# Strassen's scheme for one more product, with its weight sums spread over two engines: an attention and SiLU kernel on one core

## The chip, the cores and the metric

One core of a Trainium2 chip. The metric is the device time of one execution in microseconds (us). The changed kernel and each experiment were executed six times, beside executions of the kernel before on the same chip; medians are quoted with the lowest and the highest. Profiled spans are about 2 us shorter than the device time of the same execution.

## The reference, cut to what matters

```python
# q, k, v: (8 items, 8 heads, 576, 64), float32; w_in (512, 2048), w_out (2048, 512)
q_s = softmax(q, axis=-1)                      # over the 64 of a head
k_s = softmax(k, axis=2)                       # over the 576 positions
kv  = einsum('bhsd,bhse->bhde', k_s, v)
x   = einsum('bhsd,bhde->bhse', q_s, kv)       # -> 4608 tokens x 512
h   = x @ w_in                                 # first product
g   = h * sigmoid(h)
out = g @ w_out                                # second product
```

The 4608 tokens go through the two products in nine chunks of 512 (the first product of chunks 0 and 1 has another cut: 576 and 448 tokens). An item is 576 tokens of attention; the attention of item b stands beside chunk b-1.

## The kernel before: the parts that matter

Instructions are put at positions in a chunk by a hand-tuned table, `PLAN`, sorted, and issued in that order on each engine. Chunks 3 to 7 share one entry, `STEADY`. The first product of chunk 0 and 1 is plain; from chunk 2 on it is partly, and the second product wholly, by Strassen's scheme: seven products of half blocks in place of eight, with sums of weights (`TX` for the first product, `TW` for the second) and of activations (`XS`, `SW`) made beforehand. Second products of chunks 0 and 1 are plain:

```python
def mm2(t, i):                       # a quarter product: 4 matmuls of 128x512
    qd, tb = divmod(i, 4)
    ...
    for fc in range(qd * n, (qd + 1) * n):
        nc.tensor.matmul(out=OP[t, tb], lhsT=GT[t][:, fc, tb*128:(tb+1)*128], rhs=W2[:, fc, :], ...)
    if qd == 3:
        store(t, tb, tb % 2)

y1 = [(t, x) for t in (1, 2) for x in PLAN[t]["y"]]     # chunk 1's 16: nine in chunk 1, seven in chunk 2
for i, (t, x) in enumerate(y1):
    put(t, x, mm2, 1, i)
```

The way of one item's queries into the products: load (`lq`), exponential on ScalarE (`ex`), row sums on VectorE, normalization on GpSimd (`qnorm`), a transposition by DMA (`tp`), and then the head products on TensorE (`ox`), whose copies are the next chunk's input.

```python
put(b - 1, p["qn"][cc], qnorm, b, cc, G)                # G: GpSimd
put(b - 1, p["vs"][cc], vcast, b, cc, V if b == 1 else G)
put(b - 1, p["lq"], load, b + 1, "qt", q)               # the next item's loads and
put(b - 1, p["lk"], load, b + 1, "kt", k)               # this item's transposition and the
put(b - 1, p["lv"], load, b + 1, "vt", v)               # output stores all are issued on one
put(b - 1, p["tp"], tr_dma, b, nc.sync)                 # queue, SyncE's, in this order of positions
```

The softmax here doesn't subtract the row's maximum and nothing guards it: scores larger than these inputs give would overflow.

## Time and profile before

The kernel before took 275.68 us (median of 3; 275.18 to 276.43) and, beside the changed kernel, 276.06 us (275.18 to 277.79, six runs). Its profiled span is 274.1 us. I cut it where TensorE begins each chunk's first product; the last column ends with the last matmul, 4.9 us before the span does:

| chunk | 0 | 1 | 2 | 3 | 4 | 5 | 6 | 7 | 8 to the last matmul |
|---|---|---|---|---|---|---|---|---|---|
| before, us | 33.01 | 23.39 | 21.30 | 28.06 | 27.85 | 28.89 | 27.12 | 25.75 | 37.34 |

```profile
57.36 0.54 SPq L98 DMA_DIRECT2D qt<-in_q_dram  x1
61.71 3.30 SPq L138 DMA_TRANSPOSE qT<-eq  x1
```

The transposition of item 2 is issued at 61.71 us and lands 4.9 us later, at 66.6. So item 2's head products could not have begun before 66.6: of the 5.2 us of quarter products ahead of them, at most 2.1 us cost time.

### The profile page before, as it was taken

To read this page: it belongs to the slowest core of one execution; us is meant where nothing else is said; L and a number is where in the kernel's file an instruction comes from. 1 tells how busy PE (TensorE), PEld (TensorE's weight loads), DVE (VectorE), ACT (ScalarE), POOL (GpSimd) and SP (SyncE) were. 2 spreads that over 40 slices of the span, in tenths; PEclk is the share of its full clock that TensorE was granted. 3 is DMA by queue.
4 is the path that set the end of the run, shared out by engine and by line. 5 is a ranking of instruction groups with operands and counts; after the bars stand their busy time and mean duration, and the time that the engine had idled before them with its cause. 6 is when DMAs were issued, how large, how long until landed. Compare 5 with 4: busy or idle time off the path is not lost.

```text
span 274.1 us, 6282 instructions
## 1 busy us (share of the span) xinstructions
PE 261.6 (95%) x2546; PEld 186.8 (68%) x2546; DVE 218.1 (80%) x417; ACT 167.8 (61%) x268; POOL 70.4 (26%) x53
## 2 busy tenths in 40 slices
PE   8789999999999999999999979999999999999992
PEld 3447665444446567877787668768876887788882
DVE  2957578995786999899889988989898679687932
ACT  5646663775995798378936695499554447444300
POOL 1551080579881008001700170015200000000000
PEclk9979999999999999999999999999999999999998
DMA  7999999998707970697099707951513012201414
GB/s 249 303 193 255 324 299 179 397 333 184 301 0 162 315 284 8 130 378 248 2 129 345 275 13 146 384 200 31 117 48 79 1 41 53 66 13 28 115 41 115
DMA packets 42381, 46.48 MB, mean 170 GB/s; under 512 B 18544, under 2 KB 29808, under 8 KB 42352
## 3 DMA queue, kind: packets, MB, share of 16 engines
q1 hardware_dynamic: 37312, 38.35, 47.4%
q0 software_dynamic: 5040, 7.73, 12.6%
q8 instruction: 20, 0.33, 0.5%
q14 instruction: 9, 0.07, 0.1%
HBM read 36.70 MB, written 9.44 MB: 168 GB/s over the span
## 4 chain that ended last, share of the span: by engine, by line
PE 61%; DMA 12%; ACT 8%; DVE 8%; SPq 4%; issue 3%; POOL 2%; ACTq 0%; POOLq 0%; DVEq 0%
PE ops L410 21%; PE hps L234 16%; PE hps L317 14%; DMA kt<-in_k_dram 9%; PE ops L474 8%; DMA vt<-in_v_dram 3%; ACT ek L107 2%; SPq L98 2%; PE kvps L169 2%; SPq L463 2%; DVE u L334 2%; ACT L264 1%; ACT eq L107 1%; POOL eq L127 1%; PE o L204 1%
## 5 line engine op out<-in xcount | busy, mean ns | idle before, releaser
L234 PE MATMUL hps<-XT,W 128*128 128x512 bf16 (+3 forms) x320 | 62.9, 343 | 0.2
L410 PEld LDWEIGHTS <-GT 128*128 128x128 bf16 x448 | 43.4, 98 | 8.6 <-issue 1.0
L234 PEld LDWEIGHTS <-W 128*128 128x128 bf16 x320 | 31.6, 100 | 25.5 <-issue 1.6
L356 ACT ACTIVATE GT<-u 128x512 bf16<-128x512 f32 x40 | 25.2, 632 | 33.9 <-DVE u L334 33.9
L127 POOL TENSOR_TENSOR eq<-eq,rzq 128x1152 bf16<-128x1152 bf16 x14 | 29.6, 2132 | 35.6 <-DVE rzq L122 20.4
L317 PE MATMUL hps<-XS,TX 128*128 128x256 bf16 x240 | 34.5, 272 | 3.1 <-ACT GT L264 2.5
L317 PEld LDWEIGHTS <-TX 128*128 128x128 bf16 x320 | 31.1, 98 | 8.3 <-issue 4.4
L410 PEld LDWEIGHTS <-SW 128*128 128x128 bf16 x336 | 32.8, 98 | 4.0 <-DVE SW L370 0.2
L334 DVE SCALAR_TENSOR_TENSOR u<-hps,s 128x512 f32<-128x512 f32 x40 | 27.1, 681 | 8.7 <-PE hps L317 6.4
L260 DVE SCALAR_TENSOR_TENSOR GT<-sg,hps 128x320 bf16<-128x320 f32 (+3 forms) x64 | 24.0, 414 | 12.2 <-ACT sg L248 11.2
L474 PE MATMUL ops<-W,GT 128*128 128x512 bf16 x128 | 31.8, 379 | 0.0
L248 ACT ACTIVATE sg<-hps 128x320 f32<-128x320 f32 (+2 forms) x48 | 21.3, 456 | 15.5 <-PE hps L234 10.4
L114 POOL CAST vaug<-vt 128x1152 bf16<-128x1152 f32 x12 | 14.2, 1195 | 63.6 <-DMA vt<-in_v_dram 63.6
L334 DVE SCALAR_TENSOR_TENSOR u<-hps,u 128x512 f32<-128x512 f32 x40 | 27.3, 685 | 3.0 <-PE hps L317 2.4
L410 PE MATMUL ops<-TW,GT 128*128 128x256 bf16 x224 | 28.8, 273 | 0.0
L410 PE MATMUL ops<-W,GT 128*128 128x256 bf16 x224 | 28.7, 272 | 0.0
L410 PE MATMUL ops<-TW,SW 128*128 128x256 bf16 x224 | 28.0, 273 | 0.0
L317 PEld LDWEIGHTS <-W 128*128 128x128 bf16 x240 | 22.3, 98 | 4.8 <-issue 1.4
L121 DVE TENSOR_REDUCE zq<-eq 128x18 f32<-128x1152 bf16 x16 | 21.3, 1329 | 4.9 <-ACT eq L107 4.9
L317 PE MATMUL hps<-XT,W 128*128 128x256 bf16 x160 | 23.9, 273 | 0.0
L107 ACT ACTIVATE ek<-kt 128x1152 bf16<-128x1152 f32 x16 | 18.1, 1158 | 5.6 <-DMA kt<-in_k_dram 5.6
L224 ACT CAST XT<-o 128x512 bf16<-128x512 f32 (+3 forms) x36 | 18.3, 556 | 3.9 <-PE o L204 3.8
(69 smaller groups left out, 348.5 us busy)
## 6 DMA issues: line engine op xcount, KB each, us to landing
qt<-in_q_dram SPq DMA_DIRECT2D x6, 1152.0 KB, 6.8
kt<-in_k_dram SPq DMA_DIRECT2D x6, 1152.0 KB, 10.3
vt<-in_v_dram SPq DMA_DIRECT2D x6, 1152.0 KB, 9.2
W<-in_moe_w_in_dram POOLq DMA_DIRECT2D x4, 512.0 KB, 10.0
W<-in_moe_w_out_dram POOLq DMA_DIRECT2D x4, 512.0 KB, 17.8
out_dram<-oq SPq DMA_DIRECT2D x16, 128.0 KB, 8.5
out_dram<-u SPq DMA_DIRECT2D x30, 64.0 KB, 2.1
out_dram<-u SPq DMA_DIRECT2D x13, 128.0 KB, 2.4
```

What stands on the lines that cost most here:

```text
L107: nc.scalar.activation(out=o, in_=jgd(st[b][src], cc), func=ACT.Exp)
L121: nc.vector.reduce_sum(out=st[b]["zq"][:, cc], in_=e, axis=AX.X)
L127: eng.tensor_tensor(out=e, in0=e, in1=r[:, :, :, None].to_broadcast([128, J, 2, D]), op=ALU.mult)
L224: nc.scalar.copy(out=x, in_=o1[g][:, 0:size])
L234: nc.tensor.matmul(out=hps[:, 0:size], lhsT=W1[:, c, fb * 128:(fb + 1) * 128], rhs=XT[t][:, c, off:off + size], start=(c == 0), stop=(c == ...
L248: nc.scalar.activation(out=sg[:, 0:size], in_=hps[:, 0:size], func=ACT.Tanh, scale=0.5)
L260: nc.vector.scalar_tensor_tensor(out=y, in0=sg[:, h], scalar=1.0, in1=hps[:, h], op0=ALU.add, op1=ALU.mult)
L317: nc.tensor.matmul(out=o[:, f, :], lhsT=l(c, 2 * g + f), rhs=r(c), start=bool(first and f == 0 and c == 0), stop=(c == HK - 1), skip_group ...
L334: nc.vector.scalar_tensor_tensor(out=out, in0=o, scalar=1.0, in1=x, op0=ALU.mult, op1=ALU.add)
L356: nc.scalar.activation(out=y, in_=MP[t, g, x], func=ACT.Silu)
L410: nc.tensor.matmul(out=o[:, a, :], lhsT=l(f), rhs=r(f), start=bool(first and a == 0 and f == 0), stop=(f == HF - 1), skip_group_check=True,)
L474: nc.tensor.matmul(out=OP[t, tb], lhsT=GT[t][:, fc, tb * 128:(tb + 1) * 128], rhs=W2[:, fc, :], start=(fc == 0), stop=(fc == NFB - 1),)
```

## The change

Its intent: chunk 1's second product takes seven products of half blocks instead of eight (less work on TensorE). Since Strassen's sums need the whole chunk's activations, all of it moves into chunk 2, behind chunk 1's first product. The sums of weights are now needed earlier, so they are cut in halves and spread over VectorE and GpSimd from chunk 0 on. Every position of the plan was tuned anew with it.

```diff
-TXAT = [(0, 15.76), (0, 15.96), (1, -2.6), (1, -8.1)]
-GATE = (1, 2.8)
-TWAT = [(1, 2.4), (1, 4.9), (1, 7.9), (1, 4.9), (1, 14.95), (1, 13.95), (1, 14.95), (1, 21.95)]
+TXAT = [(0, (0, 11.76, 1, 0)), (1, (0, 15.77, 1, 0)), (2, (0, 14.78, 1, 1)), (3, (0, 15.79, 1, 1)), (0, (2, 3.1, 0, 0)), ...]
+TWAT = [(0, 10.1, 1), (0, 8.7, 1), (0, 13.0, 1), (0, 13.6, 1), (0, 14.7, 0), (0, 19.3, 1), (0, 17.9, 1), (0, 14.0, 1)]
# (chunk, position, engine: 0 VectorE, 1 GpSimd)
-    F0 = 2
+    F0 = 0
-    y1 = [(t, x) for t in (1, 2) for x in PLAN[t]["y"]]
-    for i, (t, x) in enumerate(y1):
-        put(t, x, mm2, 1, i)
-    for t in range(STD, NCH):
+    for t in range(1, NCH):
         for i, (m, a) in enumerate(HALVES):
             x = PLAN[t + 1]["y"][i]
             put(t + 1, x, product, t, m, a)
     def after(t, k):
+        c = 0.5 if t < STD else 1.0          # chunk 1's gate is (tanh + 1) h, twice the SiLU
# STEADY, chunks 3 to 7 (the rest of its positions cut)
-'lq': 10.95, 'lk': 13.9, 'lv': 11.41, 'tp': 7.9, ...
+'lq': 9.95, 'lk': 16.9, 'lv': 9.41, 'tp': 8.9, ... 'pae': [1, 0, 0], 'pbe': [0, 0, 0, 0, 1]   # two presums to GpSimd
... (PLAN[0], PLAN[1], PLAN[2], PLAN[8] re-tuned in the same way; cut)
```

## The prediction

> **What bounds the kernel now.** I read the page first (busy shares, slices, chain), then a table of the nine token chunks by stage, then the timeline of TensorE at the start of each chunk and what ended its pauses. Chunk numbers 0 to 8 are the 512-token stretches of the two products; first-product work of chunk t stands beside second-product work of chunk t-1.
>
> ```profile
> PE 261.6 (95%) x2546; PEld 186.8 (68%) x2546; DVE 218.1 (80%) x417; ACT 167.8 (61%) x268; POOL 70.4 (26%) x53
> PEclk9979999999999999999999999999999999999998
> PE 61%; DMA 12%; ACT 8%; DVE 8%; SPq 4%; issue 3%; POOL 2%; ACTq 0%; POOLq 0%; DVEq 0%
> ```
>
> TensorE is busy for 95% of 274.1 us at nearly full clock (0.7 in one early slice), so time is its column count plus its pauses. That DMA and ScalarE are in the chain at all says that there are pauses. The table by stage shows where (start:end, length, then busy time by engine):
>
> ```profile
> 16.50:49.50 33.00, 32.95 (x274) 20.19 (x272) 23.18 (x69) 19.06 (x41) 8.37 (x6) 0.95 1.13 261
> 49.50:72.90 23.40, 23.17 (x196) 10.88 (x193) 17.55 (x33) 17.07 (x28) 20.46 (x12) 1.00 0.97 316
> 72.90:94.20 21.30, 20.65 (x201) 11.91 (x200) 17.84 (x29) 16.36 (x24) 8.35 (x5) 1.00 0.53 145
> 94.20:122.30 28.10, 27.51 (x303) 21.43 (x302) 26.02 (x49) 20.95 (x33) 6.46 (x4) 1.00 0.63 199
> 122.30:150.10 27.80, 27.16 (x302) 21.39 (x300) 25.47 (x46) 19.45 (x30) 6.66 (x4) 1.00 0.65 184
> 150.10:179.00 28.90, 27.21 (x302) 21.40 (x301) 25.56 (x46) 19.51 (x30) 6.50 (x4) 1.00 0.67 214
> 179.00:206.20 27.20, 27.13 (x303) 21.50 (x302) 24.65 (x46) 19.59 (x30) 6.46 (x4) 1.00 0.35 88
> ```
>
> These are chunks 0 to 6. Chunks 3 to 6 execute the same TensorE work (302 or 303 records), yet take 28.1, 27.8, 28.9 and 27.2 us: up to 1.7 us of pause in one chunk. The cause stands in chunk 5's timelines of TensorE, ScalarE and the DMA queue:
>
> ```profile
> 160.84 0.60 PE L317 MATMUL hps<-XS,TX 128*128 128x256 bf16 x4 [1.60 <-ACT GT L264]
> 155.61 2.22 ACT L107 ACTIVATE ek<-kt 128x1152 bf16<-128x1152 f32 x2 [2.24 <-DMA kt<-in_k_dram]
> 139.61 2.73 SPq L463 DMA_DIRECT2D out_dram<-c  x4
> 142.38 0.60 SPq L98 DMA_DIRECT2D qt<-in_q_dram  x1
> 143.10 0.46 SPq L98 DMA_DIRECT2D vt<-in_v_dram  x1
> 143.60 0.51 SPq L98 DMA_DIRECT2D kt<-in_k_dram  x1
> ```
>
> The queue issues four output stores, then q, v and k. K lands about 12 us later, ScalarE has sat 2.24 us for it in front of the exponentials, the SiLU behind them frees a PSUM bank late, and TensorE waits 1.60 us.
>
> For chunk 1 I also need two rates of VectorE, and what GpSimd does to it:
>
> ```profile
> 59.30 2.38 DVE L260 SCALAR_TENSOR_TENSOR GT<-sg,hps 128x448 bf16<-128x448 f32 x4
> 72.53 2.23 DVE L276 TENSOR_TENSOR XS<-XS,XT 128x512 bf16<-128x512 bf16 x1
> 151.88 0.41 DVE L276 TENSOR_TENSOR XS<-XS,XT 128x512 bf16<-128x512 bf16 x1
> 70.08 4.40 POOL L386 TENSOR_TENSOR TW<-W 128x1024 bf16<-128x1024 bf16 x2
> ```
>
> The gating of one chunk-1 tile costs 2.38/4 = 0.595 us; the same sum takes 0.41 us alone and 2.23 us when GpSimd is in a sum of weights (70.08 to 74.5).
>
> **What the Trainium skill says.** "SBUF — State Buffer", the section on reading the port diagram, calls the pair shared by VectorE and GpSimd an exclusive lock: a VectorE operation with two SBUF inputs and a GpSimd operation that reads SBUF exclude each other for a whole instruction. The 0.41 and 2.23 us agree. It also says that one SBUF input does not contend; here the gating (one input from PSUM) keeps its pace beside GpSimd. "TensorE: Matmul & The Clock Gate", "Back-to-back issue gap", gives about N/2.4 + 2.5 ns for an isolated warm matmul and 131 ns sustained at N=512. The trace supports the first: stretches of eight 128x512 follow each other in 1.73 us (216 ns each), eight 128x256 in 0.87 us (109 ns); 131 ns is seen nowhere. "ScalarE: Activation LUTs", "What ACT_TABLE_LOAD costs", gives about 1283 ns for the load plus a drain; the trace has 1283 ns each, two around each set of exponentials.
>
> **The change part by part.**
>
> 1. Strassen for chunk 1's second product. Removed: 16 quarter products of 4 matmuls, 64 x 216 ns = 13.84 us. Added: 14 half products of 8 matmuls, 112 x 109 ns = 12.21 us. On TensorE -1.63 us.
>
> 2. Where it goes. Nine of these sixteen quarters used to fill chunk 1's own stage; now none does, all fourteen halves stand in chunk 2's. Chunk 1's stage is then TensorE 64 matmuls of 448 columns (64 x 189 ns = 12.1 us), key-value products 2 x 0.41 and head products 2 x 0.34: 13.6 us. VectorE must do 16 gatings (9.5 us), two row sums with reciprocals (2 x 1.65) and two copies of the key-value state (2 x 0.8): 14.4 us, and it starts 1.35 us in and idles about 1 us behind the first exponential. With the six-bank ring and the order of the build I followed bank by bank: the last gating ends near 16.9 us; ScalarE then has the four 0.52 us copies of the next input to finish before chunk 2 may begin, near 17.9 us, with one 0.87 us product done in between. Against 13.6 + 0.87 that is 3.4 us of pause, new.
>
> 3. Chunks 1 and 2 together. Before: TensorE's own work is 12.1 + 13.84 + 4 x 0.41 + 4 x 0.34 + 32 x 0.216 + 56 x 0.109 = 42.0 us, the stages took 44.7: 2.7 us of pauses. After: 40.3 of work, 3.4 of pause in chunk 1, an estimated 0.5 in chunk 2 (its VectorE work, about 22 us in 27, fits): 44.2. Net -0.5 us.
>
> 4. Weight sums. Four 128x1536 sums on VectorE become eight 128x1024 half-tile sums over columns 0 to 7, of which those of tiles 0 and 1 are never used; three go to GpSimd (about 2.15 us each, as the 2.17 us of the weight sums there), one of W2's goes to VectorE. GpSimd has room (8.4 of 33 us busy in chunk 0). But the first VectorE sum now stands in chunk 0 directly behind a row sum, whose result starts a 2.1 us normalization on GpSimd: the lock turns about 0.7 us into up to 2.5, and the ring holds only about two tiles of slack. I put +0.5 us on the path.
>
> 5. Steady chunks 3 to 6. Two of eight presums a chunk (0.68 us on VectorE) go to GpSimd (2.15 us). VectorE has slack there, so no direct gain. What matters is the queue: the order is now v, q, then the four stores, then k. The stores took 2.8 us, so two of three loads begin about 3 us earlier, and k, last of a 12 us burst of 3.5 MB, should land 3 us or more earlier: ScalarE's waits (1.20, 2.24, 0.47 us in chunks 4 to 6) should vanish. Chunk 3 had another reason (its table load began 2.3 us after the chunk's first matmul, 0.8 us in others), which the new end of chunk 2 mends too. Best case: chunks 3, 4, 5 fall to chunk 6's 27.1: -0.95, -0.7, -1.75 = -3.4. But both head products now stand together, 3.5 us before the chunk ends, with their copies late, so ScalarE starts its exponentials about 0.5 us later. I count -2.7.
>
> Sum: -0.5 + 0.5 - 2.7 = -2.7. From 275.68: 273.0 us.
>
> **Rivals.** (a) Only the removed columns count and chunk 1 does not starve: -1.6 - 2.7, with chunk 1's old pauses partly gone too, 270.5 to 271.5. For it: the last 16-matmul stretches show that TensorE needs no help when data is ready. Against: VectorE's 14.4 us exceed TensorE's 13.6. (b) The lock and the longer GpSimd queue bite: sums wait up to 2 us behind GpSimd at each chunk start, normalization and transposition come later, and k is late again. That eats the steady gain: 275 to 277. For it: GpSimd gets about 4.3 us more in each steady chunk. Against: it was busy only 6.5 of 28 us, and its new sums stand where the needed data come long before. (c) K is still late, since it is last in the queue after all: the steady gain is near 0 and the time 275 to 276. Against: the waits were only 0.5 to 2.2 us.
>
> **Range and chances.** The floor, with no pause from chunk 1 on, would be about 5 us under the 273.0; a gain over 2% (below 270.2) needs nearly that, 0.10. A loss over 2% (above 281.2) needs several new waits in every chunk, 0.02. Range 270.8 to 275.6.
>
> **What would show it.** Right: chunk 1's stage near 18 us with banks freed by VectorE's gating ending TensorE's pauses; chunks 1 and 2 together within 1 us of 44.2; no wait over 0.5 us of the exponentials for k; chunks 3 to 5 near 27.2 each. Wrong: chunk 1 without a pause (then rival a), pauses of 1 us or more in chunk 0 behind the weight sum, VectorE sums of 2 us at chunk starts (rival b), or k still awaited (rival c).

## More of the kernel before

Beside the lines in the prediction, one more stretch of TensorE's timeline turned out to matter, the end of chunk 1 (columns: start, duration, engine, line, operation, tiles, shapes, count; a wait, where there was one, stands in brackets at the end):

```profile
66.89 1.86 PE L234 MATMUL hps<-XT,W 128*128 128x448 bf16 x8
68.67 0.41 PE L204 MATMUL o<-qT,kvn 64*64 64x128 bf16 x8
69.02 1.04 PE L474 MATMUL ops<-W,GT 128*128 128x512 bf16 x4
69.99 0.41 PE L204 MATMUL o<-qT,kvn 64*64 64x128 bf16 x8
70.33 2.76 PE L474 MATMUL ops<-W,GT 128*128 128x512 bf16 x12
72.93 1.89 PE L234 MATMUL hps<-XT,W 128*128 128x512 bf16 x8
```

The head products (`o<-qT,kvn`) begin at 68.67 us without a wait. The first four of each group of eight are for item 1's last 128 tokens; item 2's own (64x384 in the records) follow from 68.75, and the last ends at 70.40. Quarter products fill the time around them until chunk 2 begins at 72.93 (six ahead and four beside or behind; the tenth belongs to chunk 2's plan).

## The result, and the profile after

The changed kernel took 273.03 us (271.86 to 274.37, six runs) against 276.06 us. The ratio is 0.9884, with a 95% interval of 0.9835 to 0.9933: within 2%. (Ratios are the mean time of one kernel's fast runs over that of the other's of the same rounds, so not quite the ratio of the medians that are quoted.) Executions over 1.5% slower than the fastest of the same kernel are left out of the means. The median is what was predicted. By stage it is another matter:

| chunk | before | after | difference | predicted |
|---|---|---|---|---|
| 0 | 33.01 | 32.25 | -0.76 | +0.5 |
| 1 and 2 | 44.69 | 47.20 | +2.51 | -0.5 |
| 3 to 7 | 137.67 | 132.34 | -5.33 | -2.7 |
| 8 to the last matmul | 37.34 | 37.34 | 0 | 0 |

With 0.12 us more ahead of chunk 0 and 0.09 less behind the last matmul the sum is -3.55 us, the spans' difference (274.13 to 270.58). The steps were off by -1.3, +3.0 and -2.6 us, and the errors cancelled but for 0.9: that the total was met is luck.

From the page after: engines' busy times, the clock by slices, the chain that ended last.

```profile
PE 255.8 (95%) x2580; PEld 191.9 (71%) x2594; DVE 209.8 (78%) x405; ACT 172.6 (64%) x276; POOL 110.8 (41%) x71
PEclk9999999997999999999999999999999999999998
PE 61%; DMA 14%; POOL 7%; ACT 6%; issue 5%; SPq 2%; DVE 2%; POOLq 0%; ACTq 0%
```

TensorE lost 5.8 us of busy time, GpSimd gained 40, and GpSimd entered the chain (2% to 7%). The slice at a lower clock has moved from the start to about 64 us. The table by stage, here chunks 1, 2, 4 and 5 (start:end, length, busy time of TensorE, its weight loads, VectorE, ScalarE and GpSimd with counts, granted clock, DMA share, GB/s):

```profile
48.90:69.30 20.40, 16.93 (x161) 8.54 (x160) 15.40 (x31) 14.37 (x26) 16.23 (x9) 0.92 0.98 303
69.30:96.10 26.80, 26.57 (x281) 19.50 (x281) 23.03 (x37) 21.75 (x33) 19.27 (x11) 1.00 0.74 237
...
122.60:149.80 27.20, 26.89 (x302) 21.63 (x302) 23.65 (x43) 19.52 (x31) 10.99 (x6) 1.00 0.66 215
149.80:176.40 26.60, 26.55 (x302) 21.56 (x301) 23.05 (x44) 20.39 (x32) 11.08 (x6) 1.00 0.61 183
```

Chunk 1 has 3.5 us without a matmul and a clock of 0.92; the steady chunks now run with no pause (26.55 of 26.6 us in chunk 5). Chunk 1's pauses, on TensorE's timeline:

```profile
58.43 1.67 PE L233 MATMUL hps<-XT,W 128*128 128x448 bf16 x8 [0.57 <-DVE GT L259]
62.01 0.48 PE L168 MATMUL kvps<-vaug,ek 64*64 64x65 bf16 x36 [1.91 <-POOL vaug L113]
...
63.96 2.97 PE L233 MATMUL hps<-XT,W 128*128 128x448 bf16 x8
66.86 0.25 PE L203 MATMUL o<-qT,kvn 64*64 64x128 bf16 x4
67.95 0.58 PE L203 MATMUL o<-qT,kvn 64*64 64x384 bf16 x12 [0.84 <-DMA qT<-eq]
```

Only the first pause, 0.57 us, is for VectorE's gating. The second is for GpSimd's cast of item 2's values, the third for the transposition of its queries. And eight matmuls that took 1.86 us at full clock in a repeat of this kernel (after_again, below) took 2.97, because the granted clock fell after the pauses (0.50 from 63.2 to 66.6 us):

```profile
63.00:65.00 2.00, 2.00 (x41) 1.01 (x40) 0.97 (x4) 0.54 (x1) 2.00 (x2) 0.55 1.23 222
65.00:67.00 2.00, 2.00 (x10) 0.74 (x9) 1.09 (x6) 0.58 (x2) 0.13 (x1) 0.60 1.19 165
```

The Trainium skill, "TensorE: Matmul & The Clock Gate", "What's actually happening", puts the half clock down to an idle window of about 3.4 us and has it released by about as long a stretch of work. No single pause here is that long; the first two, 0.57 and 1.91 us, lie within 4.2 us of each other's start and end, just ahead of the drop. A longer pause in another run, below, agrees with the page better.

What the cast and the transposition waited behind, on GpSimd and in the DMA queue:

```profile
56.67 4.18 POOL L126 TENSOR_TENSOR eq<-eq,rzq 128x1152 bf16<-128x1152 bf16 x2
60.81 2.24 POOL L113 CAST vaug<-vt 128x1152 bf16<-128x1152 f32 x2
```

```profile
58.03 0.54 SPq L97 DMA_DIRECT2D qt<-in_q_dram  x1
60.88 3.50 SPq L137 DMA_TRANSPOSE qT<-eq  x1
```

The transposition is issued 0.8 us earlier than before (60.88 against 61.71), but landed 7.0 us after its issue instead of 4.9: at 67.9. Compare item 2's first head product: 68.75 us before, 67.95 after. Nine quarter products, 7.8 us of TensorE work (36 x 216 ns), are gone from chunk 1, six of them from ahead of this head product, yet it comes only 0.80 us sooner, and chunk 1 itself began 0.64 sooner. What chunk 1 lost, 2.95 us, is mostly what stood beside and behind the head products. The second product's work then stands in chunk 2, which grew by 5.46 us.

In the steady chunks the queue's order is as predicted (chunk 4):

```profile
135.89 2.48 SPq L137 DMA_TRANSPOSE qT<-eq  x1
138.47 0.72 SPq L97 DMA_DIRECT2D vt<-in_v_dram  x1
139.28 0.48 SPq L97 DMA_DIRECT2D qt<-in_q_dram  x1
139.85 2.53 SPq L465 DMA_DIRECT2D out_dram<-c  x4
142.43 0.59 SPq L97 DMA_DIRECT2D kt<-in_k_dram  x1
```

and with it chunk 5's exponentials of the keys wait for nothing, while chunk 4's still wait 0.90 us:

```profile
126.53 2.22 ACT L106 ACTIVATE ek<-kt 128x1152 bf16<-128x1152 f32 x2 [0.90 <-DMA kt<-in_k_dram]
153.19 2.20 ACT L106 ACTIVATE ek<-kt 128x1152 bf16<-128x1152 f32 x2
```

In chunk 0 the weight sum on VectorE did meet GpSimd's normalization, but the other way round than feared: the sum had begun first and took 0.63 us, and the normalization beside it took 2.37 us where the one before it took 2.12. TensorE had a new wait of 0.88 us there for the last part of W2.

```profile
37.79 0.63 DVE L291 TENSOR_TENSOR TX<-W 128x1024 bf16<-128x1024 bf16 x1
...
38.01 2.37 POOL L126 TENSOR_TENSOR eq<-eq,rzq 128x1152 bf16<-128x1152 bf16 x1 [1.21 <-DVE rzq L121]
```

### The profile page after: what moved, and what is told of

Its sections match the earlier page's. It is cut to its first block, busy times and chain, and to the rows that moved or that the text cites. A ratio compares the mean times of both kernels' runs of the same rounds, so it can differ in the third digit from the quotient of the medians.

```text
span 270.6 us, 6388 instructions
## 1 busy us (share of the span) xinstructions
PE 255.8 (95%) x2580; PEld 191.9 (71%) x2594; DVE 209.8 (78%) x405; ACT 172.6 (64%) x276; POOL 110.8 (41%) x71
## 4 chain that ended last, share of the span: by engine, by line
PE 61%; DMA 14%; POOL 7%; ACT 6%; issue 5%; SPq 2%; DVE 2%; POOLq 0%; ACTq 0%
PE ops L411 30%; PE hps L316 19%; PE hps L233 8%; DMA W<-in_moe_w_out_dram 8%; DMA kt<-in_k_dram 4%; DMA qT<-eq 3%; POOL eq L126 3%; PE ops L476 2%; POOL TW L387 2%; ACT eq L106 1%; PE kvps L168 1%; ACT ek L106 1%; ACT XT L223 1%; PE o L203 1%; POOL W L516 1%
## 5 line engine op out<-in xcount | busy, mean ns | idle before, releaser
L233 PE MATMUL hps<-XT,W 128*128 128x512 bf16 (+3 forms) x312 | 61.9, 341 | 1.3 <-DVE GT L259 0.6
L411 PEld LDWEIGHTS <-GT 128*128 128x128 bf16 x512 | 50.0, 98 | 8.9 <-issue 0.2
L411 PEld LDWEIGHTS <-SW 128*128 128x128 bf16 x384 | 37.2, 98 | 5.0 <-DVE SW L371 0.2
L355 ACT ACTIVATE GT<-u 128x512 bf16<-128x512 f32 x40 | 24.5, 629 | 23.6 <-DVE u L333 23.3
L411 PE MATMUL ops<-TW,SW 128*128 128x256 bf16 x256 | 33.0, 273 | 0.0
L411 PE MATMUL ops<-W,GT 128*128 128x256 bf16 x256 | 32.9, 273 | 0.0
L411 PE MATMUL ops<-TW,GT 128*128 128x256 bf16 x256 | 32.9, 273 | 0.0
L333 DVE SCALAR_TENSOR_TENSOR u<-hps,s 128x512 f32<-128x512 f32 x40 | 27.2, 681 | 6.7 <-PE hps L316 5.3
L375 POOL TENSOR_TENSOR SW<-GT,SW 128x1024 bf16<-128x1024 bf16 x6 | 13.9, 2320 | 39.1 <-DVE SW L371 27.6
L369 POOL TENSOR_TENSOR SW<-GT 128x1024 bf16<-128x1024 bf16 x7 | 14.9, 2126 | 36.1 <-PE ops L411 36.1
L106 ACT ACTIVATE eq<-qt 128x1152 bf16<-128x1152 f32 x16 | 18.4, 1161 | 4.5 <-DMA qt<-in_q_dram 4.4
```

The costliest lines, as they stand in the source:

```text
L106: nc.scalar.activation(out=o, in_=jgd(st[b][src], cc), func=ACT.Exp)
L233: nc.tensor.matmul(out=hps[:, 0:size], lhsT=W1[:, c, fb * 128:(fb + 1) * 128], rhs=XT[t][:, c, off:off + size], start=(c == 0), stop=(c == ...
L333: nc.vector.scalar_tensor_tensor(out=out, in0=o, scalar=1.0, in1=x, op0=ALU.mult, op1=ALU.add)
L355: nc.scalar.activation(out=y, in_=MP[t, g, x], func=ACT.Silu)
L369: V.tensor_add(S1[:, f], quad(t, 0, f, 1), quad(t, 1, f, 1))
L411: nc.tensor.matmul(out=o[:, a, :], lhsT=l(f), rhs=r(f), start=bool(first and a == 0 and f == 0), stop=(f == HF - 1), skip_group_check=True,)
```

## The experiments

All runs passed the check against the reference except `no_kv2`, which is wrong. The theory after the result: the steady chunks' gain comes from the order of the DMA queue, not from Strassen's scheme; and the start (chunks 0 to 2) gains nothing, since chunk 1 ends when item 2's inputs let it. Rivals: the start helps and the queue adds little; the two presums on GpSimd, not the queue, gave the steady gain; chunk 1 merely lacks work for TensorE. The twelve runs were sent in three calls of four; the kernel before took 276.0, 276.52 and 276.22 us beside them (274.3 to 279.0 over all its runs).

### First call: which half of the change gains?

**old_start.** Chunks 0 to 2 as in the kernel before, the rest as changed.

```diff
-PLAN[0..2], TXAT, TWAT of the changed kernel; F0 = 0; chunk 1's second product by product()
+PLAN[0..2], TXAT, TWAT, GATE of the kernel before; F0 = 2; chunk 1's second product by mm2()
```

> Chunks 0 to 2 as in the kernel before (chunk 1's second product in four plain quarters, all weight sums as before), steady chunks and end as in the changed kernel. Theory A (read from the two traces: chunks 1 and 2 became 2.5 us longer, 44.7 to 47.2 us, and the whole gain, 5.1 us in chunks 3 to 6 and 0.2 in chunk 7, comes from the re-timed steady chunks): this is faster than the changed kernel by 2 to 3 us, about 270.5 us; chunks 1 and 2 together near 44.7 us, chunks 3 to 6 near 26.6 each. Rival B (Strassen on chunk 1 is worth its 1.63 us, the steady chunks gained because chunk 2 now ends otherwise): slower than the changed kernel by 1.5 us or more, 274.5 us or above.

272.62 us (271.36 to 273.84), ratio 0.9882 (0.9842 to 0.9922). The changed kernel's whole gain, without Strassen for chunk 1 and without the spread sums. Theory A's 270.5 did not come, though: chunks 1 and 2 took 44.68 us as foretold, but chunks 3 to 7 took 134.20, not 132.3.

**old_steady.** The complement: the new start, chunks 3 and on as before.

```diff
-STEADY, PLAN[8], PLAN[9] of the changed kernel
+STEADY, PLAN[8], PLAN[9] of the kernel before
```

> The complement: chunks 0 to 2 as in the changed kernel, chunks 3 to 8 timed as in the kernel before. Theory A: slower than the kernel before by about 2 us, near 278 us, with chunks 3 to 6 back at 27.1 to 28.9 us and a wait of the exponentials for k. Rival B: faster than the kernel before by 1.6 us, near 274.4.

280.76 us (278.63 to 281.84), ratio 1.0172 (1.0125 to 1.0219): 4.8 us slower than the kernel before, more than double theory A's 2 us. In the profile chunks 0 to 2 take 82.5 us (77.7 before), all of the loss, and chunk 1's transposition landed 8.1 us after its issue; chunks 3 to 7 take 137.8 us (137.7 before).

**queue_old.** The changed kernel; in the steady chunks only the three loads go back to their old positions.

```diff
-STEADY: 'lq': 9.95, 'lk': 16.9, 'lv': 9.41
+STEADY: 'lq': 10.95, 'lk': 13.9, 'lv': 11.41
```

> The changed kernel with one thing undone: in the steady chunks the loads of q, v and k stand again behind the four stores of the first output quarter. The prediction's step 5 (the order of the queue is what frees the steady chunks): k lands 3 us later, the exponentials wait for it again (over 1 us in chunks 4 and 5), the time rises by 2 to 3 us to about 275.5. Rival C (the steady gain comes from the other re-timing: presums on GpSimd, head products side by side, the end of chunk 2): within 0.7 us of the changed kernel.

279.33 us (277.26 to 281.72), ratio 1.0093 (1.0039 to 1.0148): 6.3 us slower than the changed kernel's first median, though only 2.0 above its repeat. The profile tells the two apart: chunks 3 to 7 take 137.4 us (132.3 changed), as in the kernel before (137.7), 5.1 us for three numbers in the plan. In the seven profiles here that have the changed steady chunks unaltered and the new start, these chunks take 132.0 to 132.9 us. (Chunks 1 and 2, where nothing was edited, are 4.3 us longer in this profile; the transposition landed 8.7 us after issue there.) Chunk 4, the exponentials of the keys and the pause that follows:

```profile
133.31 2.22 ACT L106 ACTIVATE ek<-kt 128x1152 bf16<-128x1152 f32 x2 [3.83 <-DMA kt<-in_k_dram]
```

```profile
138.54 0.60 PE L316 MATMUL hps<-XS,TX 128*128 128x256 bf16 x4 [3.19 <-ACT GT L263]
```

This is the prediction's chain (keys late, exponentials late, SiLU late, bank late), larger than it was before the change.

**before_queue_new.** The same three numbers the other way round, in the kernel before, and nothing else.

```diff
-STEADY: 'lq': 10.95, 'lk': 13.9, 'lv': 11.41
+STEADY: 'lq': 9.95, 'lk': 16.9, 'lv': 9.41
```

> The kernel before with one thing changed: in the steady chunks v and q are loaded ahead of the four stores and k behind them, as in the changed kernel. Step 5 of the prediction: 2 to 3 us faster than the kernel before, about 273.5, with k's waits of 1.2, 2.2 and 0.5 us gone. Rival C: within 0.7 us of the kernel before.

273.27 us (272.65 to 273.73), ratio 0.9906 (0.9869 to 0.9942). Three positions give the kernel before 2.7 us: nearly all that the whole change gives. Its chunks 3 to 7 take 134.96 us.

### Second call: what holds chunk 1, and what the presums do

**qt_behind.** The load of item 3's queries goes behind the transposition in chunk 1 instead of ahead of it.

```diff
-PLAN[1]: 'lq': 10.45
+PLAN[1]: 'lq': 11.45
```

> The changed kernel, with one load moved: in chunk 1, q of item 3 is issued behind the transposition of item 2's q, not ahead of it. Theory D (chunk 1's new pauses are the prediction's: VectorE's gating and the input copies): no change, within 0.5 us. Theory E (from three traces with the same program up to there: TensorE waited 0.84, 3.3 and 3.9 us for the transposition, which landed 7.0 to 8.7 us after its issue, behind a 1.15 MB load in the same queue): it lands about 2 to 4 us earlier, that wait is gone, and the time is 0.8 to 3 us under the changed kernel, 270.5 to 272.

272.96 us (272.53 to 273.35), ratio 0.9859 (0.9821 to 0.9898). The median is the changed kernel's. The transposition landed 6.2 us after its issue (7.0), chunk 1 took 19.36 us at full clock, and chunk 2 took 27.98, with new waits of 0.54 and 0.24 us behind ScalarE. What chunk 1 gained chunk 2 gave back. Theory E's total (270.5 to 272) missed, and TensorE's wait for the transposition was 1.35 us, not gone (0.84). Its six runs lie within 0.8 us of each other, though, the narrowest of all kernels here.

**cast_first.** GpSimd casts item 2's values before it normalizes the queries, and two weight sums go behind.

```diff
-PLAN[1]: 'vs': [9.3, 10.9];  TWAT: (0, 19.3, 1), (0, 17.9, 1)
+PLAN[1]: 'vs': [4.5, 4.6];   TWAT: (1, 11.1, 1), (1, 11.0, 1)
```

> The changed kernel, with GpSimd's order altered in chunks 0 and 1: the two casts of v of item 2 stand before its normalizations, and two half sums of W2 behind them. Theory E (the key-value product of chunk 1 waits 1.9 us for a cast that is last in GpSimd's queue, and the pause drops the granted TensorE clock to 0.55 for some 3 us, which costs about 1.5 us more): that wait and the drop are gone, 1.9 to 3.4 us less, if the transposition does not land later for it. Theory D: within 0.5 us of the changed kernel, VectorE's gating being the bound.

274.68 us (272.8 to 275.4), ratio 0.9915 (0.9870 to 0.9959). The values had not landed:

```profile
58.08 2.25 POOL L113 CAST vaug<-vt 128x1152 bf16<-128x1152 f32 x2 [5.23 <-DMA vt<-in_v_dram]
```

GpSimd sat 5.23 us for them, the normalization behind it came later, the transposition was issued at 64.51 us, and TensorE waited 3.24 us for it. The values come at 58 us whatever waits for them, so casting first was a mistake of mine.

**both_fixes.** Both edits together.

> Both of these together. Theory E: chunk 1 falls from 20.4 us to about 17 (what VectorE's gating allows by the prediction's count, 17.9 less the product that now counts to it), the time to 269 to 270.5 us, below both kernels. Theory D: 273.

275.77 us (275.21 to 277.49), ratio 0.9978 (0.9931 to 1.0025). Theory E's 269 to 270.5 us is missed clearly. The transposition landed 4.6 us after its issue, but was issued only at 64.11 us; TensorE waited 3.21 us for it, and chunk 2 took 29.11 us. The two edits do not add up.

**presum_dve.** The two presums of each steady chunk return from GpSimd to VectorE.

```diff
-STEADY: 'pae': [1, 0, 0], 'pbe': [0, 0, 0, 0, 1]
+STEADY: 'pae': [0, 0, 0], 'pbe': [0, 0, 0, 0, 0]
```

> The changed kernel, with the two presums of each of chunks 3 to 7 back on VectorE (0.68 us each in place of 2.15 us on GpSimd). The prediction's step 5 (no direct gain from this move): within 0.7 us of the changed kernel. Rival (relieving VectorE, busy 78%, is what made the steady chunks faster): 1.5 us or more slower, over 274.5, with chunks 4 to 6 above 27 us.

275.35 us (273.48 to 277.95), ratio 0.9936 (0.9886 to 0.9986). In the profile chunks 3 to 7 take 133.7 us (132.3), with small waits of TensorE for VectorE's sums in chunks 4 and 5, as this one in chunk 5:

```profile
177.48 0.60 PE L316 MATMUL hps<-XS,W 128*128 128x256 bf16 x4 [0.57 <-DVE u L333]
```

So the presums on GpSimd are worth about 1.3 us where the queue is in order, by this one profile (unaltered chunks 3 to 7 vary by 0.9 us). The total is in the rival's range (over 274.5), but not for the rival's reason alone: chunks 0 to 2 of this profile are 2.3 us longer too, without any edit there (for that see the next run).

### Third call: does chunk 1 lack work or inputs?

Theory F: the end of chunk 1 is set by the arrival of item 2's inputs. Theory G: chunk 1 only lacks work.

**after_again.** The changed kernel, unaltered.

> The changed kernel once more, unaltered. 273.0 us give or take 0.7, ratio 0.985 to 0.993, if the earlier median holds. It sizes the noise: chunk 1's length in the profile should lie between 19.5 and 23.5 us, according to when the transposition of query item 2 lands (6.2 to 8.7 us after its issue in the runs so far), with the steady chunks 3 to 7 within 0.5 us in sum of the first profile of the changed kernel.

277.36 us (273.26 to 277.99), ratio 0.9942 (0.9853 to 1.0031, from the fast runs; three of the six are called slow only because the lowest, 273.26, is over 1.5% faster). A clear miss: five of six runs lie at 277 to 278 us, above the kernel before (276.22). The profiled run:

```profile
61.10 5.44 SPq L137 DMA_TRANSPOSE qT<-eq  x1
```

```profile
70.15 0.96 PE L203 MATMUL o<-qT,kvn 64*64 64x384 bf16 x12 [4.20 <-DMA qT<-eq]
```

The transposition was issued within 0.3 us of the first profile's and landed 9.0 us later instead of 7.0; TensorE sat 4.20 us, and the clock was 0.50 from 70 to 76 us. Chunk 1 took 23.60 us (20.44), chunk 2 28.01 (26.76), chunks 3 to 7 132.41 (132.34). With 0.37 more in chunk 0 and 0.14 less ahead of it these make up the 4.7 us between the two spans. So the same program has a chunk 1 of 20 to 24 us, by when one transposition lands. Here a pause over 3.4 us brought the half clock, as the skill's section says; the release came only after some 6 us of work, not about 3.4. Why it landed later here is not known.

**filler.** Four of chunk 0's quarter products are moved into chunk 1.

```diff
+    late = {8: 10.6, 9: 11.6, 12: 12.45, 13: 13.95}
     for i, x in enumerate(PLAN[0]["y"]):
-        put(0, x, mm2, 0, i)
+        put(*((1, late[i]) if i in late else (0, x)), mm2, 0, i)
```

> The changed kernel with four of chunk 0's quarter products moved into chunk 1, so that TensorE has about 3.5 us more work there and 3.5 us less in chunk 0. Theory F (the end of chunk 1, the head product of item 2, is set by the arrival of item 2's inputs, whatever TensorE has to do before it): chunk 0 about 3.5 us shorter, chunk 1 about 3.5 us longer, the head product of item 2 at the same time of the run, 67 to 70 us, and the total within 0.7 us of the changed kernel. Theory G (chunk 1 only lacks TensorE work, the inputs are in time): the pauses of chunk 1 fill up, and the total falls by 2 to 3.5 us, to about 270.

272.37 us (271.95 to 274.13), ratio 0.9847 (0.9804 to 0.9889). Theory G's fall to 270 did not come. Of theory F's figures the total and the head product's time held, the chunks' did not: chunk 0 lost only 0.80 us, since it paused in turn, and chunk 1 gained 1.81. The lines are TensorE's pause in chunk 0 and the two groups of head products:

```profile
39.47 1.14 PE L233 MATMUL hps<-XT,W 128*128 128x320 bf16 x8 [1.75 <-DVE GT L259]
...
67.66 0.84 PE L203 MATMUL o<-qT,kvn 64*64 64x128 bf16 x10
68.66 0.75 PE L203 MATMUL o<-qT,kvn 64*64 64x128 bf16 x6 [0.16 <-DVE kvn L181]
```

With 3.5 us more work ahead of it, item 2's first head product comes at 67.78 us by the records, just after its transposition landed (67.74) and no later than in the changed kernel (67.95). The last ones wait 0.16 us for VectorE's copy of the state (`kvn`) and end at 69.40 instead of 68.53. Chunk 1 takes up 3.5 us of work for 1.8 us of length, at full clock (1.00 from 62 to 76 us), and the span is 270.6 us in both.

**no_kv2.** The keys and values of item 2 are not loaded (item 1's are used again; a wrong result).

```diff
-        for x in (("qt", q), ("kt", k), ("vt", v)):
-            load(b, *x)
+        st[b]["kt"], st[b]["vt"] = st[1]["kt"], st[1]["vt"]
+        load(b, "qt", q)
```

> The changed kernel without the loads of the keys and values of item 2 (item 1's stay in their place: a wrong result on purpose), 2.3 MB less to move while the DMA engines are fullest. Theory F: the cast of the values and the transposition no longer wait, their pauses of 1.91 and 0.84 us vanish, chunk 1 falls from 20.4 to 17 or 18 us (what VectorE's gating alone allows), and the total falls by 2.5 to 4.5 us, to 268.5 to 270.5. Rival (the order of GpSimd's own work or VectorE bounds chunk 1, not the transfers): chunk 1 stays at 19.5 or more and the total within 1 us of the changed kernel.

272.97 us (271.86 to 274.89), ratio 0.9862 (0.9815 to 0.9910). Theory F's fall to 270 did not come either; the rival's figures held (chunk 1 at 21.14 us). The wait for the cast of the values is gone, as F says, but not that for the transposition:

```profile
59.59 4.19 POOL L126 TENSOR_TENSOR eq<-eq,rzq 128x1152 bf16<-128x1152 bf16 x2 [1.37 <-ACT sg L247]
```

```profile
63.81 2.73 SPq L137 DMA_TRANSPOSE qT<-eq  x1
```

```profile
70.20 0.57 PE L203 MATMUL o<-qT,kvn 64*64 64x384 bf16 x12 [1.24 <-DMA qT<-eq]
```

The experiment was less clean than I meant it: the load of the queries was issued 1.7 us later (45.75 us, against 44.03), with eight output stores directly behind, and landed 8.5 us after its issue instead of about 6.2. So the exponential began at 54.36 us (50.77), and the normalization and the transposition came 2.9 us later than in the changed kernel. What it does show is that keys and values are not what ends chunk 1. What it leaves is a narrower theory F: the chain of the queries alone, from their load over exponential, normalization and transposition to the head products.

The ten profiles with the new start, put side by side, bear this out (from the issue and landing of item 2's transposition in each trace; us):

| | changed | qt_behind | both_fixes | no_kv2 | old_steady | cast_first | presum_dve | queue_old | after_again | filler |
|---|---|---|---|---|---|---|---|---|---|---|
| chunk 1's start to the landing | 19.01 | 17.93 | 19.78 | 19.71 | 20.17 | 19.90 | 18.76 | 21.06 | 20.98 | 19.76 |
| landing to chunk 2's start | 1.43 | 1.43 | 1.43 | 1.43 | 2.23 | 2.23 | 2.62 | 2.62 | 2.62 | 2.48 |

In all but filler TensorE sits idle for the transposition (0.84 to 4.20 us). Where the clock from the landing on is full, chunk 2 begins 1.43 us later (first four); where it is half from the landing on, 2.62; where it falls to half 0.5 us after, 2.23. So the landing ends chunk 1, and a pause or a lower clock ahead of it only fills the wait: removing the cast's pause, as cast_first and both_fixes did, could not shorten chunk 1 by itself. Whether an earlier landing alone would shorten the whole was not isolated; qt_behind's, 1.08 us earlier, did not.

**k_ahead.** The start of the kernel before and the steady chunks of the changed one (old_start), with the keys, too, ahead of the stores.

```diff
-STEADY: 'lk': 16.9
+STEADY: 'lk': 9.97
```

> The kernel with the start of the kernel before and the steady chunks of the changed one (272.62 us measured), with the load of the keys, too, put ahead of the four stores in each steady chunk: order transposition, values, queries, keys, stores. If keys are still the last thing that a steady chunk's exponentials wait for, chunk 4's wait of 0.9 us and the PE pauses after it go, and the time falls by 0.3 to 0.8 us, to about 272.0. Rival (the first change of the order has already taken all there is): within 0.3 us of 272.6. If the stores, now last, hold back the output slabs, it would be slower instead.

270.95 us (270.23 to 271.80), ratio 0.9788 (0.9748 to 0.9829): the fastest of all, 2.1% faster than the kernel before, though the interval does not exclude 2%. The gain over old_start, 1.7 us between medians of different calls, is more than expected; between the two profiles it is 0.9 us. The queue and the exponentials of the keys that it serves:

```profile
113.21 0.53 SPq L98 DMA_DIRECT2D vt<-in_v_dram  x1
113.83 0.48 SPq L98 DMA_DIRECT2D qt<-in_q_dram  x1
114.36 1.05 SPq L98 DMA_DIRECT2D kt<-in_k_dram  x1
115.51 2.59 SPq L466 DMA_DIRECT2D out_dram<-c  x4
```

```profile
125.45 2.20 ACT L107 ACTIVATE ek<-kt 128x1152 bf16<-128x1152 f32 x2
```

Old_start's wait of 0.81 us in this place is gone, TensorE's pause after it too, and chunks 4, 5 and 6 take 26.64, 26.61 and 26.60 us. In chunk 5 a wait of 0.40 us is left, with no pause of TensorE behind it. The stores, now last, hold up nothing that the profile shows. The Trainium skill, "DMA: Bandwidth & Descriptors", "Two DMAs through the same engine are not ordered", says that descriptors of one queue start in order, though they need not complete so. The runs show issue and landing only, so they do not test this: the keys are now issued 4.0 us after the transposition instead of 7.0 (110.38 to 114.36, in old_start 109.86 to 116.87), and land at 125.37 us instead of 126.02, just before the exponentials want them.

## Why the prediction was right or wrong

The total, 273.0, was met by 273.03, with step errors that cancelled: luck, as the repeat shows, whose 277.36 lies outside the range of 270.8 to 275.6. Of the four signs that the prediction named for being right only the last came, chunks 3 to 5 near 27.2 us (26.55, 27.13, 26.59). Chunk 1 was not near 18 us, chunks 1 and 2 together were 3.0 us off, and the exponentials still waited 0.90 us for keys.

**What bounds the kernel: right.** TensorE's column count and its pauses, and the steady pauses from late keys: queue_old brings them back (3.19 us), before_queue_new takes away 0.55 us of them in chunk 4 and leaves 0.45 of 1.60 in chunk 5.

**Step 1, the columns: right.** TensorE's removed work was worth -1.63 us. But it bought nothing, because of step 2.

**Step 2, chunk 1 starves: right in kind, wrong in cause.** "Near 17.9" became 20.44. VectorE's gating was named as the bound; it ended only 0.57 us of pauses, while the cast on GpSimd ended 1.91 and the transposition 0.84. Their sum, 3.3 us, is near the 3.4 foretold by chance only: it is 6.7 in the repeat. What ends the chunk is the landing of item 2's transposition, 19.0 us after the chunk's start. I had followed the banks and VectorE, and not the chain of the queries, whose transposition I would have found in the kernel before landing at 66.6 us, 2.1 us ahead of its use.

**Step 3, "Net -0.5 us": wrong, the step that failed.** Chunks 1 and 2 took 47.2 us, not 44.2; +2.5 instead of -0.5. The failed term is chunk 1's length from step 2, 2.5 us too small; chunk 2, at 26.76 against 26.3, is nearly right. The quarter products that stood in chunk 1 before were in large part free filler for a wait on item 2. Taking them away moves item 2's first head product by 0.80 us only; putting the work into chunk 2 lengthens it by 5.46. Filler shows the same from the other side: 3.5 us of work put back into chunk 1 does not make that head product later (67.78 against 67.95 us), nor the span longer. One reading in this step was wrong too: the "2.7 us of pauses" before is the stages' length less the columns, but the prediction's own table has TensorE busy for 43.8 of these 44.7 us, so pauses were 0.9. Old_start shows the sum: the old start is as fast as the new one (272.62 against 273.03). The 2.0 us that the new start loses against it in chunks 0 to 2 are made up for by chunks 3 to 7 (134.20 in old_start, 132.34 changed), chunk 3 above all, -1.28.

**Step 4, the weight sums, +0.5: wrong.** The sum on VectorE took 0.63 us; it had begun before GpSimd's normalization, which then took 0.25 us longer. Chunk 0's -0.76 is no gain of the change either, as far as the runs tell: over all profiles chunk 0 takes 31.5 to 33.2 us, full clock or not at its start (33.03 in k_ahead at full clock, 32.74 in old_start at 0.50 to 0.70), and its longest pause is mostly for W2 (0.88 us, 1.15 in k_ahead), not behind a sum.

**Step 5, the queue: right in mechanism, too small.** Chunks 3 to 7 gained 5.33 us, not 2.7. Two terms make up the difference: chunks 3, 5 and 6 fell to 26.6 and not to 27.1 (1.6 us, with another 0.2 in chunk 7), and the 0.7 us that I set aside for later exponentials was not lost. The presums on GpSimd, "no direct gain", are worth about 1.3 in chunks 4 and 5 by presum_dve, but do not explain the 26.6: chunks 3 and 6 reach it there without them. What does is not known. The keys did not land 3 us earlier either, but 0.5, 2.9 and 0.7 us (chunks 4 to 6, from each chunk's start). The point on chunk 3 held: ScalarE's table load begins 0.74 us into it (96.84 us) instead of 2.29, and old_start, with chunk 2's old end, has the 2.29 back and a chunk 3 of 27.83 us (26.55). The order of the queue in the kernel before alone gives 2.7 in both profile and time, the figure predicted; in the changed kernel its loss costs 5.1 in the profile of these chunks.

**Rivals.** (a), no starving, is refuted by 3.3 us of pauses in chunk 1. (b), the lock, cost no sum where it was put: 0.63 us in chunk 0, and sums of activations from chunk 3 on took at most 1.41 us (1.37 before). (c), keys still late, holds in small: 0.90 us in chunk 4, taken away by k_ahead for about a microsecond.

What stays open: what makes one transposition land anywhere from 4.6 to 9.0 us after its issue; why the repeat of the changed kernel was so often at 277 us; what Strassen's scheme, the spread sums and the re-tuned positions of the start are worth each, since old_start undoes all three together; and whether the normalization, put ahead of the weight sums on GpSimd, would shorten chunk 1.

## What to carry to other kernels

Before removing work from a busy engine, ask when the next thing it must wait for arrives: work that stands in front of such a wait is nearly free, and moved behind it costs full price. When one commit changes an algorithm and re-tunes the schedule, undo each part by itself: here three positions in a DMA queue gave the kernel before 2.7 of 3.0 us, and the algorithm, with the start tuned for it, nothing that could be measured. A pause ahead of a later wait costs nothing either: look for the wait that ends last. And a total that is met says little about its terms until they are compared stage by stage.

## What the Trainium skill lacked or had wrong

- "DMA: Bandwidth & Descriptors" has no figure for how far a transposition's landing scatters beside other traffic. For one and the same transposition (128x2304, bf16) the runs show 4.6 to 9.0 us from issue to landing, and 7.0 against 9.0 us in two profiles of an unaltered kernel.
- "TensorE: Matmul & The Clock Gate" speaks of an idle window of about 3.4 us. Here the granted clock fell to 0.50 for 3.4 us behind pauses of 0.57 and 1.91 us in a stage with light products between them, and not at all in qt_behind with pauses of 0.57, 1.69 and 1.35 us in the same stage; it fell after one of 3.24 us (cast_first), not after one of 3.21 (both_fixes), and at a pause of 4.20 us it was 0.50 until 6 us of work were done. The page has no measure for how short idles add up.
- The same page's 131 ns sustained for N=512 was again seen nowhere; 216 ns was.
